# An attention and two-layer FFN kernel on one core: GpSimd's multiplication by 1/sum split by head, and a new table of order offsets

## The chip, the core and the metric

The kernel runs on one core of a Trainium2 chip. The metric is the device time of one execution in microseconds (us). A core has five engines that run side by side: TensorE (PE in the profile; its weight loads are listed as PEld), VectorE (DVE), ScalarE (ACT), GpSimd (POOL) and SyncE (SP), which issues nearly all DMAs here. Each engine takes its instructions strictly in the order of its own queue, so one that waits also holds back everything behind it.

## What is computed

Windowed attention with a few always visible first positions ("sinks"), and behind it two FFN blocks on the 1536 resulting rows. Cut to what matters:

```python
B, H, S, D = 2, 8, 768, 64;  n_sink, window = 4, 128
scores = q @ k.transpose(0, 1, 3, 2) / sqrt(D)
keep = (pos_key < n_sink) | ((0 <= pos_q - pos_key) & (pos_q - pos_key < window))
a = exp(where(keep, scores, -1e9) - max)
a = a / (sum(a) + 1e-9)
x = (a @ v).transpose(0, 2, 1, 3).reshape(1536, 512)
h = x @ w_in1;  g = h if h >= 1, 0 if h <= -1, else (h + 1)**2 / 4;  y = g @ w_out1
h = y @ w_in2;  g = relu(h)**2;  out = g @ w_out2        # d_ff = 2048
```

## The kernel before

**Attention units.** The attention is cut into 24 units (b, j, c): batch b, a block of 256 query rows j = 0..2, a pair of heads c = 0..3. In the names of tiles the numbers are these three, then u (which half of 128 rows) and e (which head of the pair): `p_1_3_0` is the tile p of unit j = 1, c = 3, half u = 0, and holds both heads. A unit goes through these steps:

- SP loads q and k for two units at a time, and v (line 579). PE transposes k and q of a unit into the single PSUM bank `turns` (`turn`, line 660), DVE copies that out as tile k (`turn_copy`, line 674). The next unit can be transposed only when the copy is done. SP moves the last 128 keys of the row block before into place (line 639).
- PE multiplies q by k for each half and head (`scores`, line 690, tiles `s` and `bank`). DVE adds the mask and finds the extreme of each row (`least`, line 699), ACT takes the exponential and the row sum (`powers`, line 707), DVE adds 1e-9 and takes the reciprocal for all four half-and-head sums of the unit (`norm`, lines 713 and 714).
- POOL multiplies the exponentials by 1/sum (`weigh`, line 721), one instruction for a half, over both heads: 2 x 260 columns, or 2 x 128 for the first half of a batch. For j > 0 it then picks the four sink columns out of the product (`sink_cols`, lines 726 and 729).
- PE transposes the product for each head (`turn_p`, line 738, tile `tx`), ACT copies it out (line 745, tile `pt`); the sink columns go the same way (`turn_s`, tile `ts`, lines 751 and 758). PE multiplies by v (line 776, tile `av`), and ACT and DVE write the result into x as a high and a low part (lines 782 and 786).

**FFN.** Every product is done in three matmuls on parts of the operands split into high and low. Weights arrive as 512 KB loads (tile `wraw`, lines 266 and 271). ACT (lines 287, 291, 308), DVE (304, 305, 297, 307) and POOL (309) turn each into its two parts, tile `w`. Hidden products (line 375) go through DVE, ACT and POOL (line 408, tile g) and then into the output products (line 451). While the attention runs, the first FFN steps are mixed in between.

**What sets the order.** `Planner.run` replays the whole program as tasks with costs (`COST`), latencies (`LAG`), waits between kinds of matmuls on PE (`SWITCH`) and buffers (`SLOTS`). At each step it takes the task that can begin first; between tasks that could begin at the same time the smaller key goes first. A key is the unit's number plus an offset for its kind (`KEYS`), plus an entry of `ADJUST` for that one task, by its number. The instructions are then written out in that order, engine by engine. So one changed entry can move many instructions.

Of the kernel before, what the change touches and what calls it, by code (L numbers as in the profile page):

```python
# [17 lines left out]
P = 128  # L18
# [25 lines left out]
    q=2, v=VB, k=KB, p=PB, pt=PTB, sm=4, sp=2, st=2, vs=1, sc=SCB, tp=TPB, tx=TXB, f=PSF,  # L44
# [4 lines left out]
    q=-147.90, v=245.47, kd=-117.22, kp=-240.89, tp=276.69, tpc=83.42, kp0=96.04, s0=-29.55,  # L49
# [12 lines left out]
LEAD = 336.00, 31.97  # L62
LAG = dict(PE=53, ACT=33, DVE=33, POOL=78, SP=40)
COST = dict(
    q=("SP", 2200, 0, 2320), v=("SP", 1100, 0, 1160), kd=("SP", 500, 0, 230), wi=("SP", 500, 0, 1470),
    wo=("SP", 500, 0, 1270), vs=("SP", 900, 0, 200), od=("SP", 500, 0, 800),
    kp=("POOL", 139, 189, 0), kp0=("POOL", 139, 189, 0), vsm=("POOL", 470, 515, 0),
    pm=("POOL", 1006, 1056, 0), pms=("POOL", 562, 615, 0), sp=("POOL", 280, 345, 0),
    cl=("POOL", 1225, 1280, 0), gl=("POOL", 690, 740, 0), gl5=("POOL", 1240, 1290, 0),
    yl=("POOL", 690, 740, 0), yl5=("POOL", 1240, 1290, 0),  # L70
    go=("DVE", 0, 500, 0), gp=("PE", 0, 100, 0),
# [13 lines left out]
)  # L85
FRONT = 137
ADJUST = {
# [4 lines left out]
}  # L92
KIND = dict(s=0, ss=0, tp=1, x=1, xx=6, ts=1, av=2, avv=3, mm=4, mm5=4, vc=5, vl=5)
TAIL = dict(n=92, e=60, es=60, mm5=30)
SWITCH = (
# [3 lines left out]
)  # L99
# [32 lines left out]
class Planner:  # L132
# [5 lines left out]
    def add(self, kind, key, emit, after=(), takes=(), uses=(), count=0, behind=None):  # L138
        n = len(self.tasks)
        t = Task(kind, (key + ADJUST.get(n, 0), n), emit, after, list(takes), list(uses), count)  # L140
        for h in t.uses:
            h.left += 1
        for d in t.after:
            d.next.append((t, False))
        if behind:
            t.after = t.after + [behind]
            behind.next.append((t, True))
        self.tasks.append(t)
        return t
# [439 lines left out]
class Attention:  # L589
# [123 lines left out]
        self.nc.vector.tensor_scalar(sm[:, 1], sm[:, 1], 1.0e-9, None, ALU.add)  # L713
        self.nc.vector.reciprocal(sm[:, 2], sm[:, 1])  # L714

    def weigh(self, b, j, c, u):
        st = self.st[b, j, c]
        wid = P if j + u == 0 else WIN
        s = st["p", u][:, :, :wid]
        r = st["sm"][:, 2, u].unsqueeze(2).broadcast_to([P, 2, wid])  # L720
        self.nc.gpsimd.tensor_tensor(s, s, r, ALU.mult)  # L721

    def sink_cols(self, b, j, c, u):
# [69 lines left out]
    def plan(self, line):  # L793
        add, hold = line.add, Hold
        raw, val, keyh, sinks, self.mask_tasks = {}, {}, {}, {}, {}
        u = {}
        for n, unit in enumerate(UNITS):
# [66 lines left out]
            sp, stt, av = hold("sp"), hold("st"), hold("tx")  # L864
            for i in range(2):
                small = "s" if j + i == 0 else ""
                pm.append(add("pm" + small, key(f"pm{i}"), at(self.weigh, i), [norm], [], [sm]))
                if j > 0:
                    cols.append(
                        add("sp", key(f"sp{i}"), at(self.sink_cols, i), [pm[-1]], [sp][i:], [ph[i]])  # L870
                    )
            turned, ptu = [], []
            few = "x" if j == 0 else ""
            for e in range(2):
                h, pt = hold("tx"), hold("pt")
                t = add(few + "x", key(f"x{e}"), at(self.turn_p, e), pm, [h], ph)
                turned.append(add(few + "xc", key(f"xc{e}"), at(self.turn_p_copy, e), [t], [pt], [h]))
                ptu.append(pt)
            if j > 0:
# [75 lines left out]
def plan_ffn(line, ffn, weights, stage, wtmp, units):  # L955
# [5 lines left out]
    for n, key in enumerate([key for chunks in PASSES for key in chunks]):  # L961
        ps = [key in chunks for chunks in PASSES].index(True)
        raw, ring = [Hold("wr"), Hold("wr")], Hold("w")
        rings[key] = ring
        load = LOADS[n] if n < EARLY else first[ps] - LEAD[0] + 0.1 * PASSES[ps].index(key)
        part = PARTS[n] if n < EARLY else first[ps] - LEAD[1] + 0.1 * PASSES[ps].index(key)
        step = 0.3 if n < EARLY else 0.05
        loads = []
        for h in range(2):
            f = lambda k=key, h=h: weights.load(k, h, stage)  # L970
            before = add("wo" if h else "wi", load + 0.01 * h, f, [before], [raw[h]])
            loads.append(before)
        for h in range(2):
            tmp, last = Hold("wt"), loads[h]
            for i, (kind, f) in enumerate(weights.parts(key, h, wtmp, ring)):
                takes = ([tmp] + [ring] * (h == 0)) if i == 0 else []
                uses = [tmp] * (kind == "cl") + [raw[h]] * (kind in ("ca", "c3"))
                after = [last, begin] if i == 0 else [last]
                after = [last, low] if kind == "c4" else [high] if kind == "c1" else after
                last = add(kind, part + step * h + 0.001 * i, f, after, takes, uses)  # L980
                high, low = last if i == 0 else high, last if i == 1 else low
                begin = last if i == 0 else begin
            parts[key, h] = last
# [358 lines left out]
```

## Time and profile before

| | |
|---|---|
| three runs | 638.45, 639.63, 639.88 us; median 639.63 |
| the profiled execution | 639.68 us, of which the profile's span is 637.6 us |
| TensorE's granted clock | 0.998 of full speed, mean over the span |
| busy share of the span | PE 98%, PEld 80%, DVE 64%, ACT 51%, POOL 48% |
| the chain that ended last | PE 92%, ACT 2%, DVE 2%, POOL 1%, DMA 1% |

How it is read: a share is a mean over stages that differ. The attention of batch 0 lies between about 10 and 65 us, that of batch 1 is mixed with FFN work up to about 173 us, and the rest is FFN alone. A PE that counts as busy may still have waited inside the pipeline, so the times from one start to the next are compared as well.

### The profile page before, as it was taken

The page shows a single profiled execution, that of the slowest core. Times are in us where ns is not written, and L with a number is a line of the kernel's source. Part 1 is how long each engine was busy: PE and PEld are TensorE (multiplying, and loading weights), DVE is VectorE, ACT ScalarE, POOL GpSimd, SP SyncE. Part 2 cuts the span into 40 slices and gives each one's busy share as a digit, 9 for nine tenths or more (in the row PEclk, how much of TensorE's full clock was granted, in tenths as well). Part 3 has the DMA queues.
Part 4 walks back from the last instruction along what each step waited for, and adds up shares of the span by engine and source line. Part 5 has one row for each costly group of instructions (what it writes and reads, how often), then busy time and mean ns, then how long its engine had stood idle before and what let it go on. Part 6 is the DMA issues. An engine that isn't in the chain of part 4 may idle for free.

```text
span 637.6 us, 9207 instructions
## 1 busy us (share of the span) xinstructions
PE 627.8 (98%) x3254; PEld 512.4 (80%) x3254; DVE 410.3 (64%) x855; ACT 324.8 (51%) x695; POOL 305.1 (48%) x334
## 2 busy tenths in 40 slices
PE   8989999999999999999999999999999999999996
PEld 7667788887888887888888888888888888888885
DVE  6888997744478776685498886565664555222222
ACT  4899877654455553554355654555454244211320
POOL 5599487363343543542448873544354144212311
PEclk9999999999999999999999999999999999999999
DMA  6876712300022323223122222223222120001012
GB/s 148 202 202 156 198 50 93 84 1 2 10 89 67 99 67 95 70 67 99 34 67 68 66 67 72 94 67 99 79 87 67 36 96 1 2 1 49 17 66 72
DMA packets 63901, 47.89 MB, mean 75 GB/s; under 512 B 39653, under 2 KB 58341, under 8 KB 63845
## 3 DMA queue, kind: packets, MB, share of 16 engines
q1 hardware_dynamic: 62466, 46.56, 25.5%
q10 hardware_dynamic: 1378, 0.66, 0.4%
q8 instruction: 27, 0.44, 0.3%
q14 instruction: 30, 0.24, 0.1%
HBM read 43.01 MB, written 3.15 MB: 72 GB/s over the span
## 4 chain that ended last, share of the span: by engine, by line
PE 92%; ACT 2%; DVE 2%; POOL 1%; DMA 1%; issue 0%; SPq 0%; DVEq 0%; POOLq 0%; ACTq 0%
PE h L375 25%; PE o L451 20%; PE bank L451 15%; PE bank L375 12%; PE turns L451 7%; PE av L776 3%; PE s L690 3%; PE tx L738 3%; PE turns L375 3%; PE turns L660 1%; ACT p L707 1%; DMA wraw<-in_moe_w_in_dram 1%; PE ts L751 1%; PE bank L899 1%; POOL g L408 0%; DVE p L699 0%
## 5 line engine op out<-in xcount | busy, mean ns | idle before, releaser
L408 POOL TENSOR_TENSOR g<-u,g 128x512 fp32r<-128x512 f32 (+1 forms) x102 | 133.2, 1310 | 168.1 <-ACT g L404 125.5
L375 PE MATMUL h<-x,w 128*128 128x512 f32 x732 | 170.8, 389 | 0.0
L375 PEld LDWEIGHTS h<-x,w 128*128 128x128 f32 x732 | 137.4, 188 | 28.6
L309 POOL TENSOR_TENSOR w<-wx,w 128x512 fp32r<-128x512 f32 x64 | 82.6, 1291 | 123.5 <-ACT w L308 114.6
L404 ACT CAST g<-u 128x512 fp32r<-128x512 f32 (+1 forms) x102 | 60.4, 594 | 58.4 <-DVE u L390 32.3
L375 PE MATMUL bank<-x,w 128*128 128x512 f32 (+1 forms) x420 | 86.9, 356 | 0.0
L308 ACT CAST w<-wx 128x512 fp32r<-128x512 f32 x64 | 39.7, 620 | 81.0 <-DVE wx L307 81.0
L375 PEld LDWEIGHTS bank<-x,w 128*128 128x128 f32 x420 | 69.4, 189 | 11.6 <-DVE u L382 0.3
L304 DVE TENSOR_SCALAR wx<-wx 128x512 f32<-128x512 f32 x64 | 39.6, 619 | 49.7 <-ACT wx L287 49.2
L451 PE MATMUL o<-w,g 128*128 128x512 f32 (+1 forms) x288 | 70.5, 385 | 0.0
L451 PE MATMUL o<-g,w 128*128 128x512 f32 x273 | 67.6, 390 | 0.2 <-POOL g L408 0.2
L451 PE MATMUL bank<-g,w 128*128 128x512 f32 (+1 forms) x324 | 66.2, 345 | 0.0
L451 PEld LDWEIGHTS o<-w,g 128*128 128x128 f32 x288 | 53.4, 188 | 11.3 <-POOL g L408 0.5
L287 ACT ACTIVATE wx<-wraw 128x512 f32<-128x512 f32 x64 | 42.7, 667 | 37.7 <-POOL w L309 36.1
L451 PEld LDWEIGHTS o<-g,w 128*128 128x128 f32 x273 | 51.1, 188 | 11.3 <-POOL g L408 0.6
L451 PEld LDWEIGHTS bank<-g,w 128*128 128x128 f32 x324 | 51.8, 189 | 8.4 <-issue 0.5
L307 DVE CUSTOM_DVE_ANT_0 wx<-wx,wy 128x1024 uint16<-128x1024 uint16 x64 | 56.0, 875 | 2.6
L721 POOL TENSOR_TENSOR p<-p,sm 128x520 f32<-128x520 f32 (+1 forms) x48 | 48.5, 1027 | 18.2 <-DVE sm L714 9.8
L388 ACT ACTIVATE u<-u,half 128x512 f32<-128x512 f32 (+1 forms) x54 | 36.2, 674 | 37.1 <-DVE u L382 37.0
L297 DVE SCALAR_TENSOR_TENSOR wx<-wraw,wx 128x512 int32<-128x512 int32 x64 | 54.2, 847 | 1.1
L490 DVE TENSOR_TENSOR acc<-o,acc 128x512 f32<-128x512 f32 (+1 forms) x50 | 30.0, 605 | 34.7 <-PE o L451 34.6
L390 DVE SCALAR_TENSOR_TENSOR u<-h,u 128x512 f32<-128x512 f32 x37 | 25.4, 687 | 37.5 <-ACT u L384 37.5
(105 smaller groups left out, 853.2 us busy)
## 6 DMA issues: line engine op xcount, KB each, us to landing
wraw<-in_moe_w_in_dram SPq DMA_DIRECT2D x32, 512.0 KB, 3.7
wraw<-in_moe_w_out_dram SPq DMA_DIRECT2D x32, 512.0 KB, 3.5
vr<-in_v_dram SPq DMA_DIRECT2D x24, 128.0 KB, 3.6
qr<-in_q_dram SPq DMA_DIRECT2D x22, 128.0 KB, 3.0
kr<-in_k_dram SPq DMA_DIRECT2D x22, 128.0 KB, 2.8
out_dram<-acc SPq DMA_DIRECT2D x10, 256.0 KB, 2.0
k<-k SPq DMA_DIRECT2D x16, 64.0 KB, 2.1
qr<-in_q_dram SPq DMA_DIRECT2D x4, 64.0 KB, 2.7
```

The costliest lines, as they stand in the source:

```text
L287: nc.scalar.activation(s["x"], f32(s["r"][:, :, 1]), AF.Abs, scale=65536.0)
L297: nc.vector.scalar_tensor_tensor(s["xi"], s["r"][:, :, 1], -(1 << 31), s["xi"], ALU.bitwise_and, ALU.bitwise_or)
L304: ("c1", lambda: nc.vector.tensor_scalar(s["x"], s["x"], 2.0, None, ALU.max)),
L307: ("c4", lambda: nc.vector.tensor_tensor(s["xi"], s["xi"], s["yi"], ALU.add)),
L308: ("cc", lambda: nc.scalar.copy(s["w"][:, 0], s["x"])),
L309: ("cl", lambda: nc.gpsimd.tensor_tensor(s["w"][:, 1], s["x"], f32(s["w"][:, 0]), ALU.subtract)),
L375: nc.tensor.matmul(s["h"], w[:, a, c * P : (c + 1) * P], x[:, b, c, sl], start=n == 0, stop=n == 11)
L388: nc.scalar.activation(s["u"], s["u"], AF.Square, bias=self.half, scale=0.5)
L404: nc.scalar.copy(halves()[0], s["u"])
L408: nc.gpsimd.tensor_tensor(g[1], s["u"], f32(g[0]), ALU.subtract)
L451: nc.tensor.matmul(s["o"], lhs, rhs, start=n + i + j == 0, stop=n == len(chunks) - 1 and i == 1)
L721: self.nc.gpsimd.tensor_tensor(s, s, r, ALU.mult)
```

## The change

Two things are done. `weigh` becomes one POOL instruction for each half and each head (128 x 260 or 128 x 128), with costs to match (569 and 347 ns for the planner where it had 1006 and 562 for two heads). The transposition of head e now waits for the products of head e in both halves, no longer for those of both heads; `sink_cols` waits for both heads of its half. And the planner's numbers change: the first weight load is a kind of its own, `wi0`, whose landing is set 1000 ns later than before; one entry of `SWITCH` goes from 0 to -98; and `ADJUST` has 79 entries where it had 28, all but five of them for tasks of the attention.

```diff
-    pm=("POOL", 1006, 1056, 0), pms=("POOL", 562, 615, 0), sp=("POOL", 280, 345, 0),
+    pm=("POOL", 569, 620, 0), pms=("POOL", 347, 400, 0), sp=("POOL", 280, 345, 0),
...
+    wi0=("SP", 500, 0, 2470),
...
 ADJUST = {
-    209: 325.8, 243: -535.7, 259: -670.5, 348: -90, 353: -1079.1, 387: -240.3, 401: 34.6,
...
+    48: 394.2, 59: 830.871, 74: 1068.43, 96: -879.888, 97: -1091.35, 99: 257.872, 117: 334.328,
...
 SWITCH = (
-    (0, 0, 0, 10, 102, 0, 0, 0), (96, 28, 0, 115, 28, 0, 25, 0), (90, 100, 0, 0, 185, 0, 90, 0),
+    (-98, 0, 0, 10, 102, 0, 0, 0), (96, 28, 0, 115, 28, 0, 25, 0), (90, 100, 0, 0, 185, 0, 90, 0),
...
-    def weigh(self, b, j, c, u):
+    def weigh(self, b, j, c, u, e):
         st = self.st[b, j, c]
         wid = P if j + u == 0 else WIN
-        s = st["p", u][:, :, :wid]
-        r = st["sm"][:, 2, u].unsqueeze(2).broadcast_to([P, 2, wid])
+        s = st["p", u][:, e, :wid]
+        r = st["sm"][:, 2, u, e : e + 1].broadcast_to([P, wid])
         self.nc.gpsimd.tensor_tensor(s, s, r, ALU.mult)
...
             for i in range(2):
                 small = "s" if j + i == 0 else ""
-                pm.append(add("pm" + small, key(f"pm{i}"), at(self.weigh, i), [norm], [], [sm]))
+                for e in range(2):
+                    own = key(f"pm{i}") + 0.001 * e
+                    pm.append(add("pm" + small, own, at(self.weigh, i, e), [norm], [], [sm]))
                 if j > 0:
                     cols.append(
-                        add("sp", key(f"sp{i}"), at(self.sink_cols, i), [pm[-1]], [sp][i:], [ph[i]])
+                        add("sp", key(f"sp{i}"), at(self.sink_cols, i), pm[-2:], [sp][i:], [ph[i]])
                     )
...
-                t = add(few + "x", key(f"x{e}"), at(self.turn_p, e), pm, [h], ph)
+                t = add(few + "x", key(f"x{e}"), at(self.turn_p, e), pm[e::2], [h], ph)
...
-            before = add("wo" if h else "wi", load + 0.01 * h, f, [before], [raw[h]])
+            before = add("wo" if h else "wi" if before else "wi0", load + 0.01 * h, f, [before], [raw[h]])
```

PE, DVE, ACT and SP issue the same instructions as before in another order; POOL issues 48 more. On PE the first 24 rows and the last 1024 (of some 2000) stand as before. The lines of the changed kernel are 9 to 11 higher.

Place 1, POOL, around the products of unit j = 2, c = 0 of batch 0 (line 721, then 730). Before:

```order
L309 TENSOR_TENSOR w_0_580<-wx_0_1_712,w_0_580 128x512
L721 TENSOR_TENSOR p_2_0_1_777<-p_2_0_1_777,sm_2_0_722 128x520
L721 TENSOR_TENSOR p_2_0_0_723<-p_2_0_0_723,sm_2_0_722 128x520
L726 CAST sink_p_252<-p_2_0_1_777 128x2x8
L729 TENSOR_TENSOR sink_p_252<-p_2_0_1_777,sink_p_252 128x8
```

And in the change:

```order
L318 TENSOR_TENSOR w_0_551<-wx_0_1_710,w_0_551 128x512
L730 TENSOR_TENSOR p_1_3_0_604<-p_1_3_0_604,sm_1_3_603 128x260
L658 COPY k_0_1_829<-k_0_1_829 128x4
L735 CAST sink_p_255<-p_1_3_1_750 128x2x8
L738 TENSOR_TENSOR sink_p_255<-p_1_3_1_750,sink_p_255 128x8
L730 TENSOR_TENSOR p_2_0_0_766<-p_2_0_0_766,sm_2_0_765 128x260
L730 TENSOR_TENSOR p_1_3_0_604<-p_1_3_0_604,sm_1_3_603 128x260
L730 TENSOR_TENSOR p_2_0_1_809<-p_2_0_1_809,sm_2_0_765 128x260
L735 CAST sink_p_255<-p_1_3_0_604 128x2x8
```

The two products of two heads are now four of one, and those of the units c = 3 of block 1 and c = 0 of block 2 are mixed.

Place 2, PE, from the scores of unit c = 2 to those of unit c = 3 (block 0, batch 0). Before:

```order
L690 MATMUL s_0_2_0_1_343<-k_0_2_329 128x128
L660 MATMUL turns<-ident,kr_0_2_263 128x128 x2
L660 MATMUL turns<-ident,qr_0_2_260 128x128 x2
L738 MATMUL tx_0_0_0_357<-ident,p_0_0_0_280 128x128
L738 MATMUL tx_0_0_0_357<-ident,p_0_0_1_296 128x128 x2
L738 MATMUL tx_0_0_1_366<-ident,p_0_0_0_280 128x128
L738 MATMUL tx_0_0_1_366<-ident,p_0_0_1_296 128x128 x2
L690 MATMUL bank_64<-k_0_2_329 128x260
L690 MATMUL bank_65<-k_0_2_329 128x260
L690 MATMUL s_0_3_0_0_388<-k_0_3_364 128x128
```

And in the change:

```order
L699 MATMUL s_0_2_0_1_344<-k_0_2_329 128x128
L747 MATMUL tx_0_0_0_349<-ident,p_0_0_0_280 128x128
L747 MATMUL tx_0_0_0_349<-ident,p_0_0_1_296 128x128 x2
L669 MATMUL turns<-ident,kr_0_2_263 128x128 x2
L669 MATMUL turns<-ident,qr_0_2_260 128x128 x2
L747 MATMUL tx_0_0_1_367<-ident,p_0_0_0_280 128x128
L747 MATMUL tx_0_0_1_367<-ident,p_0_0_1_296 128x128 x2
L699 MATMUL s_0_3_0_0_389<-k_0_3_382 128x128
L699 MATMUL s_0_3_0_1_391<-k_0_3_382 128x128
L669 MATMUL turns<-ident,kr_1_0_271 128x128 x2
```

Between the four transpositions of unit c = 3 into `turns` and its first scores there were six transpositions and two scores; now there are three transpositions.

Place 3, SP and ACT, at the first weight load. SP before, and then in the change:

```order
L639 DMA k_2_0_440<-k_1_0_309 128x128
L579 DMA qr_2_0_448<-in_q_dram 128x4x64 x2
L579 DMA kr_2_0_451<-in_k_dram 128x4x64 x2
L266 DMA wraw_0_0_481<-in_moe_w_in_dram 128x4x256
L579 DMA vr_1_2_492<-in_v_dram 128x4x64 x2
```

```order
L648 DMA k_2_0_432<-k_1_0_309 128x128
L275 DMA wraw_0_0_443<-in_moe_w_in_dram 128x4x256
L588 DMA qr_2_0_449<-in_q_dram 128x4x64 x2
L588 DMA kr_2_0_452<-in_k_dram 128x4x64 x2
L588 DMA vr_1_2_482<-in_v_dram 128x4x64 x2
```

ACT before, up to the instruction that reads this load, and then in the change:

```order
L707 ACTIVATE p_1_1_1_526,sm_1_1_510<-p_1_1_1_526,sm_1_1_510 128x260
L782 CAST x<-av_0_2_528 128x256
L707 ACTIVATE p_1_1_1_526,sm_1_1_510<-p_1_1_1_526,sm_1_1_510 128x260
L745 COPY pt_0_3_0_557<-tx_0_3_0_537 128x384
L745 COPY pt_0_3_1_570<-tx_0_3_1_542 128x384
L707 ACTIVATE p_1_1_0_511,sm_1_1_510<-p_1_1_0_511,sm_1_1_510 128x260
L287 ACTIVATE wx_0_0_581<-wraw_0_0_481 128x512
```

```order
L754 COPY pt_0_2_0_519<-tx_0_2_0_504 128x384
L716 ACTIVATE p_1_1_0_540,sm_1_1_539<-p_1_1_0_540,sm_1_1_539 128x260
L296 ACTIVATE wx_0_0_552<-wraw_0_0_443 128x512
L791 CAST x<-av_0_1_527 128x256
L300 ACTIVATE wy_0_0_564<-wraw_0_0_443 128x512
L754 COPY pt_1_0_0_572<-tx_1_0_0_556 128x512
L754 COPY pt_0_2_1_580<-tx_0_2_1_521 128x384
```

On SP the load goes ahead of the q and k loads of block 2. On ACT the instruction that reads it goes ahead of eight: three exponentials, three copies to `pt` and two casts to x.

## Rows read from the trace of the kernel before

**Rows 1.** The page's first part: busy time and share of the engines.

```profile
PE 627.8 (98%) x3254; PEld 512.4 (80%) x3254; DVE 410.3 (64%) x855; ACT 324.8 (51%) x695; POOL 305.1 (48%) x334
```

**Rows 2.** Busy time by stretch: from:to, length, PE, PEld, DVE, ACT, POOL, clock, DMA share, GB/s.

```profile
10.00:26.00 16.00, 15.71 (x126) 11.42 (x125) 14.43 (x65) 14.09 (x55) 9.73 (x17) 1.00 0.73 169
26.00:39.00 13.00, 11.75 (x96) 8.25 (x96) 10.39 (x40) 11.51 (x36) 9.82 (x22) 1.00 0.88 226
39.00:58.00 19.00, 17.45 (x140) 12.93 (x138) 16.62 (x55) 17.30 (x51) 17.36 (x31) 1.00 0.61 150
58.00:100.00 42.00, 42.00 (x338) 34.21 (x337) 38.64 (x121) 35.21 (x104) 28.77 (x42) 1.00 0.52 134
```

**Rows 3.** Timeline of PE at its waits: start, length, instruction, idle before, released by.

```profile
26.41 0.72 PE L690 MATMUL s<-k 64*128 64x260 f32 x4
27.06 0.66 PE L738 MATMUL tx<-ident,p 128*128 128x128 f32 x4
27.55 0.41 PE L751 MATMUL ts<-ident,sink_p 128*96 128x128 f32 x2
27.80 0.60 PE L738 MATMUL tx<-ident,p 128*128 128x128 f32 x4
29.10 0.44 PE L660 MATMUL turns<-ident,kr 128*128 128x128 f32 x2 [0.70 <-DVE k L674]
...
31.13 0.71 PE L690 MATMUL s<-k 64*128 64x260 f32 x4
32.23 0.66 PE L738 MATMUL tx<-ident,p 128*128 128x128 f32 x4 [0.39 <-POOL p L721]
...
40.48 0.71 PE L690 MATMUL s<-k 64*128 64x260 f32 x4
41.72 0.44 PE L660 MATMUL turns<-ident,kr 128*128 128x128 f32 x2 [0.53 <-DVE k L674]
...
45.77 0.71 PE L690 MATMUL s<-k 64*128 64x260 f32 x4
47.13 0.66 PE L738 MATMUL tx<-ident,p 128*128 128x128 f32 x4 [0.65 <-POOL p L721]
...
239.88 0.50 PE L451 MATMUL o<-g,w 128*128 128x512 f32 x1 [0.21 <-POOL g L408]
```

**Rows 4.** Timeline of POOL, the two products of unit j = 2, c = 0.

```profile
45.01 2.07 POOL L721 TENSOR_TENSOR p<-p,sm 128x520 f32<-128x520 f32 x2
```

**Rows 5.** Groups by form, POOL line 721: busy us, mean ns, idle before, releasers.

```profile
L721 POOL TENSOR_TENSOR p<-p,sm 128x520 f32<-128x520 f32 x40 | 43.6, 1105 | 16.5 <-DVE sm L714 8.1 <-ACT p L707 3.5 <-ACT pt L745 2.9
L721 POOL TENSOR_TENSOR p<-p,sm 128x256 f32<-128x256 f32 x8 | 5.1, 636 | 1.7 <-DVE sm L714 1.7
```

**Rows 6.** Line 721 alone by stretch: POOL's busy time, count, clock, DMA.

```profile
26.00:39.00 13.00, 5.44 (x6) 1.00 0.88 226
39.00:58.00 19.00, 8.57 (x8) 1.00 0.61 150
```

**Rows 7.** Groups by form, DVE's copy out of the bank `turns`.

```profile
L674 DVE COPY k<-turns 128x512 f32<-128x512 f32 x23 | 15.7, 685 | 0.8 <-PE turns L660 0.7
```

**Rows 8.** Timeline of ACT ahead of the first weight.

```profile
24.17 0.52 ACT L707 ACTIVATE p<-p,sm 128x260 f32<-128x260 f32 x1
...
24.68 0.84 ACT L745 COPY pt<-tx 128x384 f32<-128x384 f32 x2
...
27.30 0.68 ACT L287 ACTIVATE wx<-wraw 128x512 f32<-128x512 f32 x1 [1.28 <-DMA wraw<-in_moe_w_in_dram]
```

**Rows 9.** SP's issues (timeline), the load's time in the chain, and its size (DMA issues).

```profile
20.03 1.10 SPq L579 DMA_DIRECT2D qr<-in_q_dram  x2
...
22.52 4.76 DMA wraw<-in_moe_w_in_dram
...
wraw<-in_moe_w_in_dram SPq DMA_DIRECT2D x32, 512.0 KB, 3.7
```

More of the change, by code (lines that the diff above doesn't have):

```diff
@@ L64 @@
 COST = dict(
-    q=("SP", 2200, 0, 2320), v=("SP", 1100, 0, 1160), kd=("SP", 500, 0, 230), wi=("SP", 500, 0, 1470),
+    q=("SP", 2200, 0, 2320), v=("SP", 1100, 0, 1160), kd=("SP", 500, 0, 230), wi=("SP", 500, 0, 1470), wi0=("SP", 500, 0, 2470),
     wo=("SP", 500, 0, 1270), vs=("SP", 900, 0, 200), od=("SP", 500, 0, 800),
     kp=("POOL", 139, 189, 0), kp0=("POOL", 139, 189, 0), vsm=("POOL", 470, 515, 0),
-    pm=("POOL", 1006, 1056, 0), pms=("POOL", 562, 615, 0), sp=("POOL", 280, 345, 0),
+    pm=("POOL", 569, 620, 0), pms=("POOL", 347, 400, 0), sp=("POOL", 280, 345, 0),
     cl=("POOL", 1225, 1280, 0), gl=("POOL", 690, 740, 0), gl5=("POOL", 1240, 1290, 0),
```

15 rows, old and new, of the table ADJUST are left out of this document.

## The prediction

> **What bounds the kernel now.** I read the busy shares first: PE is busy for 627.8 us, 98% of the span, and DVE, the next after PE's own weight loads, for 64% [rows 1]. So PE sets the end, and as PE issues the same instructions before and after, only PE's waits can change. The busy time by stretch then says where these lie: PE idles 0.29 us in 10 to 26, 1.25 us in 26 to 39 and 1.55 us in 39 to 58, 3.09 us in all, and nothing from 58 to 100 [rows 2]. In the same stretches ACT is busy 89% and 91%, and POOL 91% in the last: the attention of batch 0 is a pipeline whose stages are nearly all full, so a late step has little room to be made up. The timeline of PE shows each wait and what ended it [rows 3]. Idle time alone tells too little, since the matmul before a wait is still ending; so I take start to start. Two scores that wait for nothing take 0.65 us to the next start (26.41 to 27.06), four transpositions 0.49 us (27.06 to 27.55). The four long waits are then:
>
> - 27.80 to 29.10: 1.30 - 0.49 = 0.81 us, for DVE's copy out of `turns`
> - 31.13 to 32.23: 1.10 - 0.65 = 0.45 us, for POOL's products
> - 40.48 to 41.72: 1.24 - 0.65 = 0.59 us, for DVE's copy
> - 45.77 to 47.13: 1.36 - 0.65 = 0.71 us, for POOL's products
>
> These are 2.56 us. Their idle parts (0.70, 0.39, 0.53, 0.65) are 2.27 of the 3.09 us, so small waits hold another 0.82 us. One more stands in the FFN, 0.21 us of idle time at 239.88. **The ceiling of the gain is 2.56 + 0.82 + 0.21 = 3.59 us**, 0.6% of the time.
>
> **The change, part by part.**
>
> *Products by head, seen by PE.* At 45.01 POOL runs two products of two heads in 2.07 us, and PE begins the transposition of head 0 only when both are done, at 47.13 [rows 3, 4]. Of four products by head, the first two are enough. A product of 520 columns takes 1105 ns and one of 256 takes 636 [rows 5]: a line through both gives 1.78 ns a column and 0.18 us fixed, so 0.64 us for 260. Head 0 is then ready about 2 x 0.64 = 1.29 us after the start, 0.78 us earlier. That covers both POOL waits: **-1.16 us** (0.45 + 0.71), between 0 (if the products themselves begin later) and -1.16.
>
> *Products by head, paid on POOL.* 48 more starts of 0.18 us are 8.7 us of POOL time over the first 173 us. From 58 us on POOL is busy 28.8 of 42 us and PE never idles, which hides them. Between 39 and 58 us eight products are split, 8 x 0.18 = 1.44 us, and POOL's idle time there is 19.00 - 17.36 = 1.64 us: it just fits, and nothing else is left to cover it [rows 2, 6]. The same in 26 to 39: 6 x 0.18 = 1.1 us into 3.2 us. I take **+0.4 us**; bounds 0 and 2.5 (both in full on the path).
> The Trainium skill's GPSIMD Engine Reference, section 3.1 (elementwise cycle accounting), prices a two-operand product at some 2.6 cycles an element, 4497 ns for 2048 elements, and names a software dispatch for each instruction without a figure. By elements alone a split costs nothing, and this term would be zero. The two rows of different width contradict a price by elements alone, and I go by them.
>
> *The order of `turns`.* Both DVE waits come from transposing the next unit into the one bank before the last was copied out; in the new order those two places are other pairs, so 0.81 + 0.59 = 1.40 us go. New ones come: in place 2 the first scores of unit c = 3 stand three transpositions behind the four that fill `turns`. PE needs about 7 x 0.12 = 0.86 us for these seven (0.49 for four), while the scores need the four and then DVE's copy, 0.49 + 0.685 = 1.18 us [rows 7], and DVE is seldom free at once: a new wait of 0.3 us or more, I take 0.5. Further on the new order has two pairs of refills that are closer together than most; I allow 0.4 us. Net **-0.5 us**, bounds -1.4 and +0.3.
>
> *The first weight.* ACT waits 1.28 us for it at 27.30 [rows 8]. It was issued at 22.52 and took 4.76 us; in the new order it is issued where the q load stood, at 20.03, so it lands at 24.8 at the latest, or 23.7 with the median of 3.7 us [rows 9]. But ACT also gets there earlier: three exponentials at 0.51 and three copies at 0.42 no longer stand ahead, 2.8 us less than 26.02, so 23.2 or earlier [rows 8]. ACT then still waits 0.5 to 1.6 us, with other exponentials queued behind it. So I take **0**, bounds -0.8 and +0.3: the wait is moved, not removed.
>
> *What the load passes on SP.* The q and k loads of block 2 are issued 0.55 us later and behind 512 KB, which at 226 GB/s are 2.3 us of the DMA engines' time [rows 2, 9]. PE transposes them at about 26 us. I take **+0.4 us**, bounds 0 and 2.3.
>
> *All other waits* (0.82 + 0.21 us) end in ACT copies, POOL's sink columns and a g of the FFN. All get new neighbours; I take half: **-0.5 us**, bounds -1.0 and +0.5.
>
> Sum: -1.16 + 0.4 - 0.5 + 0 + 0.4 - 0.5 = -1.36 us. Against the profiled execution's 639.68 us that gives **638.3 us**. The median of the runs shown, 639.63, is the same within 0.05.
>
> **The rivals.**
>
> *Nearly all waits go.* The load's passing costs nothing, POOL's extra starts fit, and the new neighbours are better ones. For it: the waits are few and each has a single cause. Against it: ACT and DVE stay as full as they were. The ceiling leaves 639.7 - 3.6 = 636.1; I put this case at 636.4.
>
> *The waits only move.* ACT is 91% busy in 39 to 58 [rows 2], none of its work is removed, and its wait for the weight stays. What PE no longer waits for from POOL it then waits for from ACT a few steps later. The offsets change the order and not the time: 639.6.
>
> *POOL becomes the bound (slower).* Place: 26 to 58 us. 14 products are split there, 14 x 0.18 = 2.5 us [rows 6]. It decides as soon as POOL's idle time between 39 and 58 us, 1.64 us, is used up, for instance because products begin later than before. Then the gain of 1.16 us doesn't come, the starts are on the path and each delays the sinks behind it: +2.5 - 0.5 + 0.4 = +2.4, so 642.1. Against it: 0.2 us are still free, and PE no longer needs the second pair at once.
> The Trainium skill's Perfetto Trace Analysis, "Optimizing Scalar/DVE Operations", speaks of other engines but has both sides of this: group work into larger operations on a saturated engine, and break instructions up where an unsaturated one causes bubbles elsewhere. Taken over to a POOL that is 91% busy, the first half would speak for this rival; the two POOL waits of PE speak for the second half. No row of the kernel before decides it.
>
> **How the numbers follow.** A measurement of this kernel tells changes from about 0.2%, 1.28 us, so faster means below 638.35. The forecast has a chance of 0.55, with its own range 637.0 to 639.3, a good half of it (0.31) below 638.35. Nearly all waits gone 0.15, waits only moved 0.15, POOL the bound 0.15. Faster: 0.31 + 0.15 = 0.46; within 0.2%: 0.24 + 0.15 = 0.39; slower: 0.15. The range of 8 in 10 takes in the forecast, the moved waits and parts of the outer cases: 636.2 to 641.0.
>
> **What would show it.** In the profile after, PE should idle less than 3.09 us between 10 and 58 us, with no wait of `tx` for POOL over 0.3 us; a wait of `s` for DVE's copy near 14 us would confirm place 2; ACT should still wait for the first weight, by 0.5 to 1.6 us near 24; POOL should be busy about 8 us more in all, and over 95% between 39 and 58 us. I am wrong if PE's transpositions of block 2 wait for their loads by more than 1 us, if POOL waits for nothing there and PE for POOL, or if new waits stand in the FFN behind 173 us, where the order moved too.

## The result, and the profile after

| | before | after |
|---|---|---|
| runs | 638.45 to 639.88 us (4) | 642.89 to 643.09 us (4) |
| median | 639.68 us | 643.00 us |
| the profiled execution | 639.68 us | 643.09 us |
| its span, mean granted clock | 637.6 us, 0.998 | 641.0 us, 0.998 |

The change makes the kernel **slower by 3.3 us**: the ratio is 1.0058, with a 95% interval from 1.0046 to 1.0070. The prediction was 638.3 us with a range of 636.2 to 641.0. Sign and range were both wrong; the rival "POOL becomes the bound" (642.1) came nearest.

The first part of the page after, to be held against [rows 1]:

```profile
PE 630.3 (98%) x3254; PEld 512.2 (80%) x3254; DVE 415.7 (65%) x855; ACT 327.1 (51%) x695; POOL 312.4 (49%) x382
```

POOL has its 48 more instructions and 7.3 us more work (312.4 - 305.1). PE has 2.5 us more (630.3 - 627.8) **for the same 3254 instructions**: three quarters of the loss stands in the profile as busy time, not as idle time. (A second profile of the kernel before has 627.0, so 0.8 us of such a difference can be chance.) The busy time by stretch (columns as in [rows 2], and 100 to 173 besides) shows the same from the other side:

```profile
10.00:26.00 16.00, 15.14 (x113) 10.62 (x111) 14.52 (x60) 12.55 (x46) 10.75 (x26) 1.00 0.78 186
26.00:39.00 13.00, 12.11 (x96) 8.10 (x93) 11.88 (x39) 11.93 (x38) 10.74 (x25) 1.00 0.93 231
39.00:58.00 19.00, 18.50 (x151) 13.70 (x152) 16.52 (x55) 17.83 (x54) 17.00 (x35) 1.00 0.56 147
58.00:100.00 42.00, 41.80 (x338) 34.17 (x335) 36.89 (x115) 35.69 (x105) 32.08 (x56) 1.00 0.48 124
100.00:173.00 73.00, 72.42 (x483) 57.31 (x482) 44.98 (x128) 43.00 (x111) 40.05 (x73) 1.00 0.15 43
```

PE idles 0.86 + 0.89 + 0.50 = 2.25 us from 10 to 58 us, less than the 3.09 before, as forecast. The 0.20 and 0.58 us behind that make the sum 3.03: as much as before. Idle time alone would call this kernel equal.

The waits of PE, by what ended them (engine, tile and line; total us, times, longest). The first line is the start of the program and is in every profile here:

```profile
PE bank L910 <- POOL ident masks.py:199: 1.7, 1, 1.7
PE s L699 <- DVE k L683: 0.9, 2, 0.6
PE tx L747 <- POOL p L730: 0.5, 2, 0.3
PE tx L747 <- ACT pt L754: 0.4, 1, 0.4
PE ts L760 <- POOL sink_p L738: 0.4, 1, 0.4
PE o L460 <- POOL g L417: 0.3, 1, 0.3
PE av L785 <- ACT sink_t L767: 0.3, 1, 0.3
PE bank L699 <- DVE sm L708: 0.2, 1, 0.2
```

The two long waits for products [rows 3] are gone; no `tx` waits over 0.3 us for POOL. In their place stand waits for DVE, ACT and the sink columns.

From 170.45 us on before, and from 172.59 in the changed kernel, PE has the same number of matmuls left, 2046, all of the FFN. Up to some 356 us they stand in another order, from there in the same. Counted from the end, the changed kernel is 2.14 us late at the first of them, 1.9 us at 356 us, 2.80 us at PE's last matmul (635.60 against 632.80), and 3.4 us at the end of the span. So **about 2.1 us are lost in the attention**, 0.7 in the FFN, and 0.6 behind PE's last matmul. A loss in the FFN needs no new order: all nine other kernels below that keep PE's order of before lose 0.36 or 0.37 us at one and the same output product (337.26 us in the kernel before), those too that are ahead of it there.

To see the waits that a pipelined PE hides I took, in 10 to 173 us, the time from start to start of each pair of successive matmuls, less the time of the fastest fifth of pairs of the same two kinds in all profiles of this study. Steps more than 0.1 us over that, whose releaser the trace names, add up to (sums of the unrounded figures):

| us, ended by | DVE | ACT | POOL | sum | median time |
|---|---|---|---|---|---|
| before | 3.3 | 1.0 | 1.6 | 5.9 | 639.7 |
| after | 4.4 | 1.4 | 2.0 | 7.8 | 643.0 |
| split in the old order | 2.1 | 0.8 | 4.4 | 7.3 | 642.2 |
| small POOL instructions added | 3.5 | 0.7 | 3.7 | 7.9 | 642.8 |
| split, low sink part left out | 3.6 | 1.2 | 1.2 | 5.9 | 639.5 |
| after, addition left out | 2.9 | 2.4 | 0.7 | 5.9 | 641.3 |
| fitted order, two heads, 2nd | 3.8 | 0.0 | 0.2 | 4.0 | 634.8 |

The 1.9 us between the first two rows are nearly all of the 2.14. But how a step is put down to an engine matters: if only the waits of the matmul itself count, and not those of the weight load ahead of it, the POOL column stays the same within 0.1 us, while DVE has 2.3 before and 2.3 after, ACT 0.4 and 1.3, and the sum rises by 1.3 us. So POOL's column can be leaned on, DVE's rise of 1.1 us cannot.

The other rows are the experiments that follow. Ratios there are to the kernel before on the same chip, and each has its own runs of it (medians 638.96 to 639.38).

### The profile page after: what moved, and what is told of

It is laid out like the page before. It is cut to its first block, busy times and chain, and to the rows that moved or that the text cites. A ratio compares the mean times of both kernels' runs of the same rounds, so it can differ in the third digit from the quotient of the medians.

```text
span 641.0 us, 9251 instructions
## 1 busy us (share of the span) xinstructions
PE 630.3 (98%) x3254; PEld 512.2 (80%) x3254; DVE 415.7 (65%) x855; ACT 327.1 (51%) x695; POOL 312.4 (49%) x382
## 5 line engine op out<-in xcount | busy, mean ns | idle before, releaser
L384 PE MATMUL h<-x,w 128*128 128x512 f32 x696 | 162.1, 389 | 0.0
L384 PEld LDWEIGHTS h<-x,w 128*128 128x128 f32 x696 | 130.7, 188 | 27.1
L384 PE MATMUL bank<-x,w 128*128 128x512 f32 (+1 forms) x492 | 104.1, 361 | 0.1
L384 PEld LDWEIGHTS bank<-x,w 128*128 128x128 f32 x492 | 82.9, 189 | 15.6 <-issue 0.8
L460 PE MATMUL o<-w,g 128*128 128x512 f32 (+1 forms) x300 | 73.6, 386 | 0.3 <-POOL g L417 0.3
L460 PE MATMUL o<-g,w 128*128 128x512 f32 x279 | 70.5, 389 | 0.0
L730 POOL TENSOR_TENSOR p<-p,sm 128x260 f32<-128x260 f32 (+1 forms) x96 | 59.8, 647 | 18.3 <-DVE sm L723 16.0
L460 PE MATMUL bank<-g,w 128*128 128x512 f32 (+1 forms) x300 | 60.0, 341 | 0.0
L460 PEld LDWEIGHTS bank<-g,w 128*128 128x128 f32 x300 | 47.2, 189 | 7.6 <-DVE acc L497 0.7
L716 ACT ACTIVATE p<-p,sm 128x260 f32<-128x260 f32 (+1 forms) x96 | 47.0, 493 | 8.0 <-DVE sm L708 7.5
```

What stands on the lines that cost most here:

```text
L384: nc.tensor.matmul(s["h"], w[:, a, c * P : (c + 1) * P], x[:, b, c, sl], start=n == 0, stop=n == 11)
L460: nc.tensor.matmul(s["o"], lhs, rhs, start=n + i + j == 0, stop=n == len(chunks) - 1 and i == 1)
L716: self.nc.scalar.activation(s, s, AF.Exp, bias=sm[:, 0, u, e : e + 1], scale=-1.0, accum_out=sm[:, 1, u, e : e + 1])
```

## The experiments

**1. The split alone, in the old order.** In `weigh` of the kernel before:

```diff
-        s = st["p", u][:, :, :wid]
-        r = st["sm"][:, 2, u].unsqueeze(2).broadcast_to([P, 2, wid])
-        self.nc.gpsimd.tensor_tensor(s, s, r, ALU.mult)
+        for e in range(2):
+            s = st["p", u][:, e, :wid]
+            r = st["sm"][:, 2, u, e : e + 1].broadcast_to([P, wid])
+            self.nc.gpsimd.tensor_tensor(s, s, r, ALU.mult)
```

> The kernel before with one edit: each product of two heads is written as two products of one head at the same place; no order, offset or cost is changed. Theory P (POOL is the bound in the attention: each extra start of 0.18 us makes POOL's products and sink columns later, and that is the whole loss): slower than before by 2 to 3.5 us, 641.7 to 643.2 us. Theory O (the split is about neutral and the new offsets are a worse order): within 1 us of before, 638.7 to 640.7, and the prediction's own terms for the split alone (-1.16 + 0.4) would give 638.9.

Measured: 642.23 us, ratio 1.0051 (1.0031 to 1.0072). **The split alone costs 3.3 us**, as theory P said. The order of every engine is that of before, so each matmul can be compared with itself. PE's timeline:

```profile
46.21 0.66 PE L739 MATMUL tx<-ident,p 128*128 128x128 f32 x4 [1.09 <-POOL p L722]
46.70 0.38 PE L660 MATMUL turns<-ident,kr 128*128 128x128 f32 x2
46.92 0.38 PE L660 MATMUL turns<-ident,qr 128*128 128x128 f32 x2
48.74 0.42 PE L752 MATMUL ts<-ident,sink_p 128*96 128x128 f32 x2 [1.44 <-POOL sink_p L730]
```

and POOL's:

```profile
44.19 2.72 POOL L722 TENSOR_TENSOR p<-p,sm 128x260 f32<-128x260 f32 x4
46.86 0.66 POOL L727 CAST sink_p<-p 128x16 fp32r<-128x16 f32 x1
47.59 0.20 POOL L730 TENSOR_TENSOR sink_p<-p,sink_p 128x8 f32<-128x8 f32 x1
47.74 0.66 POOL L727 CAST sink_p<-p 128x16 fp32r<-128x16 f32 x1
48.48 0.20 POOL L730 TENSOR_TENSOR sink_p<-p,sink_p 128x8 f32<-128x8 f32 x1
```

The same `ts` before, and the sink columns ahead of it on POOL:

```profile
48.43 0.42 PE L751 MATMUL ts<-ident,sink_p 128*96 128x128 f32 x2 [0.21 <-POOL sink_p L729]
...
47.02 0.40 POOL L726 CAST sink_p<-p 128x16 fp32r<-128x16 f32 x1
47.49 0.20 POOL L729 TENSOR_TENSOR sink_p<-p,sink_p 128x8 f32<-128x8 f32 x1
47.64 0.46 POOL L726 CAST sink_p<-p 128x16 fp32r<-128x16 f32 x1
48.17 0.20 POOL L729 TENSOR_TENSOR sink_p<-p,sink_p 128x8 f32<-128x8 f32 x1
```

At the first `tx` of the split PE is 0.92 us ahead of [rows 3] (47.13), and POOL begins its four products 0.82 us ahead of [rows 4] (45.01). They take 2.72 us where the pair took 2.07, and the sink columns end at 48.68, where they ended at 48.37. PE needs them for `ts`, which before began at 48.43 and now at 48.74. The lead is gone at one step: **the wait for the products has become a wait for the sink columns behind them.** Of the 1.13 us by which POOL's chain is longer there, 0.65 are the products; the rest is in the two casts, 0.66 us each where they took 0.40 and 0.46, for a reason that no run here shows. Further losses of 0.59 us (a `tx` at 58.32, for products) and 0.32 us (a `ts` at 113.56) end in POOL too. In this profile PE's last matmul is 1.6 us late, and 1.1 us more lie behind it; those are not waits for POOL (last section).

**2. Head 0 first.** The changed kernel's tasks with the orders of before, written out as a list that the planner must follow, and in 15 units the products in the order head 0, head 0, head 1, head 1:

```diff
                 for t in tasks:
+                    if t.key[1] != given[e][0]:
+                        continue
                     at = self.starts(t, free)
```

> The changed kernel's tasks (products by head, head e transposed after its own two products) in the order of the kernel before on every engine; where the two halves' products stand next to each other on POOL (15 of 24 units) they go head 0, head 0, head 1, head 1. Theory P: POOL has the same 48 starts, so it is as slow as the split in the old order, within 0.5 us (641.7 to 643.2). The prediction's mechanism (head 0 ready 0.78 us earlier ends PE's two waits for POOL): at least 0.8 us faster than the split in the old order.

Measured: 642.20 us, ratio 1.0044 (1.0031 to 1.0057): no faster than the first, so the prediction's mechanism doesn't pay even where head 0 goes ahead in both halves. The waits of PE say why:

```profile
PE ts L898 <- POOL sink_p L876: 2.4, 2, 2.2
...
PE tx L885 <- POOL p L868: 0.3, 1, 0.3
```

The waits for products are 0.3 us (1.0 before) and those for sink columns 2.4 (0.2 before). The `ts` that began at 48.43 before, and at 48.74 in experiment 1, begins at 49.26 here. What follows on it differs from experiment 1, since in this profile the clock falls behind that wait (last section).

**3. Head 0 first where PE waited, and nowhere else.** In `weigh` of the kernel before:

```diff
+        parts = [(u, slice(0, 2))]
+        if (b, j, c) in ((0, 1, 1), (0, 2, 0)):
+            parts = [(1, slice(0, 1))] if u else [(0, slice(0, 1)), (1, slice(1, 2)), (0, slice(1, 2))]
+        for u, e in parts:
```

> The kernel before with products by head in two units alone, those for which PE waited for POOL before (j = 1, c = 1 and j = 2, c = 0 of batch 0), in the order head 0, head 0, head 1, head 1; 4 extra starts, 0.7 us of POOL. The prediction's mechanism alone (both waits of PE for products vanish): 1.16 us faster, 637.8 to 638.5. If PE then waits for the sink columns of the same unit instead: within 0.5 us of before.

Measured: 639.83 us, ratio 1.0007 (0.9996 to 1.0017): no gain. This run shows the term of the prediction and its undoing side by side, in PE's timeline:

```profile
31.71 0.66 PE L742 MATMUL tx<-ident,p 128*128 128x128 f32 x4
32.97 0.39 PE L780 MATMUL av<-sink_t,vs 96*128 96x256 f32 x1 [0.61 <-ACT pt L749]
...
46.33 0.66 PE L742 MATMUL tx<-ident,p 128*128 128x128 f32 x4
...
49.09 0.42 PE L755 MATMUL ts<-ident,sink_p 128*96 128x128 f32 x2 [1.67 <-POOL sink_p L733]
```

Both `tx` start without a wait. Against the same matmuls before, PE gains 0.46 us at the first and 0.72 us at the second: 1.18 us, where the prediction had 1.16. A step later the first 0.45 us go to a wait for ACT's copy, and 2.8 us later 1.46 us go to the sink columns.

**4. POOL's time without the split.** A copy of 4 columns on a tile of its own behind each of the 48 products of two heads:

```diff
         self.nc.gpsimd.tensor_tensor(s, s, r, ALU.mult)
+        self.nc.gpsimd.tensor_copy(self.pad[:, 4:8], self.pad[:, :4])
```

> The kernel before, products of two heads, with one more small POOL instruction (a copy of 4 columns on a tile of its own, no data of the kernel) behind each of the 48 products: as many extra POOL starts as the split has, about 0.14 to 0.19 us each by the rows of the 4 and 8 column copies, but nothing of the split's earlier head 0. Theory P (the extra POOL time in the attention is the loss): 2 to 4 us slower than before. If something else of the split costs (its waits, its order): within 1 us of before.

Measured: 642.76 us, ratio 1.0048 (1.0031 to 1.0065). POOL's groups by form (busy us, mean ns, idle before) give the copies:

```profile
L724 POOL COPY pad<-pad 128x4 f32<-128x4 f32 x48 | 14.3, 299 | 0.0
```

and the page's first part POOL's sum:

```profile
PE 630.1 (98%) x3254; PEld 513.6 (80%) x3254; DVE 412.0 (64%) x855; ACT 326.0 (51%) x695; POOL 312.3 (49%) x383
```

POOL is busy 312.3 us, as in the changed kernel (312.4), and the time is the same. The copies took 299 ns where 140 to 190 were expected, 14.3 us in all; the sum rose by 7.2 only, because other POOL rows were shorter. So **POOL's time alone, 7 us more of it spread over the attention, is enough for a loss as large as that of the split**; its waits and its order are not needed to explain it. Part of the loss came by way of the clock (last section). The Trainium skill's GPSIMD Engine Reference gives in section 3.1 a price per element and, for the dispatch of an instruction on GpSimd, no figure. The copies of 4 columns take 299 ns here, which a price per element alone would miss.

**5. POOL's time given back.** The second instruction of `sink_cols` is taken out, in three kernels:

```diff
-        self.nc.gpsimd.tensor_tensor(t[:, 1], p, t[:, 0], ALU.subtract)
```

In the split with the old order:

> The split in the old order, without the second instruction of the sink columns (the low part of the sink weights is left out): POOL has the 48 extra starts (8.7 us) and 32 instructions less (6.7 us). Theory P: most of the loss of the split goes, 638.5 to 640. If POOL's time is not the cause: it stays above 641.5.

In the kernel before and in the changed kernel:

> The kernel before without the second instruction of the sink columns (the low part of the sink weights is left out, 32 POOL instructions, 6.7 us of POOL time by the row of 210 ns each); the order of all else is kept. Theory P: POOL is not the bound before, so the gain is small, 0 to 1.2 us (638.5 to 639.7). Theory O: the same gain as in the changed kernel, whatever it is.

> The changed kernel without the second instruction of the sink columns (the same part left out, 32 POOL instructions, 7.8 us of POOL time at 244 ns each), order kept. Theory P: this gives POOL back about what the split took, so most of the loss goes: 2 us or more faster than the changed kernel, 639.8 to 641.0, and the gap to the kernel before without the same instruction closes to under 1.5 us. Theory O: the gap stays near 3.3 us.

Measured: 639.52 us, ratio 1.0000 (0.9990 to 1.0010), for the split: its loss is gone. The kernel before gains little (638.43; 0.9989, 0.9980 to 0.9999). But the **changed kernel gains 0.8 us and no more** (642.24; 1.0046, 1.0029 to 1.0062, which overlaps with the 1.0046 to 1.0070 that it had): theory P, as far as it was to explain the changed kernel, was wrong there. With POOL relieved, the new order is 2.7 us slower than the old one with the same split (642.24 against 639.52). So POOL's time is not what holds most of the loss in the new order. (The instruction taken out stands itself in the chain to the sink columns, as the added starts and copies do; these runs don't tell POOL's total time from the length of that chain.) The table above points to what does: against the split in the old order, the new order has brought POOL's share down from 4.4 to 2.0 us, and DVE's and ACT's up from 2.9 to 5.8 (from 1.4 to 3.6 without the waits of weight loads).

**6. Time off DVE.** That was then tried: the addition of 1e-9 to the row sums is left out.

```diff
-        self.nc.vector.tensor_scalar(sm[:, 1], sm[:, 1], 1.0e-9, None, ALU.add)
```

> The changed kernel without the addition of 1e-9 to the row sums (24 DVE instructions of 128x4, 5.4 us of DVE in the rows; that addition is left out). Theory D (in the new order PE's waits that end in DVE and ACT hold the loss; giving POOL back 7.8 us brought only 0.8): 1 us or more faster than the changed kernel, 640.5 to 642. If the loss there is neither POOL's nor DVE's: within 0.5 us of it.

> The split in the old order, without the same addition. There POOL bounds, and DVE is not what PE waits for (its waits for POOL are twice those for DVE): theory D expects less than in the changed kernel, 0 to 0.8 us, 641.4 to 642.3. A gain as large as in the changed kernel would speak against it: the addition also stands in the chain ahead of POOL's products.

> The kernel before without the same addition, as the base of the two others: 0 to 1 us faster than before, 638.4 to 639.4.

Measured: the changed kernel 641.27 us (1.0030, 1.0018 to 1.0041), 1.7 us less than with it; the split in the old order 642.27 (1.0045, 1.0028 to 1.0061), unchanged; the kernel before 638.86 (0.9997, 0.9988 to 1.0007). So the two slow kernels are not slow for the same reason: **in the old order POOL binds; in the new one the chain through DVE holds more than POOL's own time does.** Whether it is DVE's time stays open: the addition also stands in the chain ahead of POOL's products, and in the table POOL's share falls by 1.3 us along with DVE's 1.5, while ACT's rises by 1.0. The profile of the split without the addition shows the fall of the clock (last section), that of experiment 1 doesn't; this may hide a small gain, but not one of 1.7 us, as the fastest runs, 641.51 and 641.76, lie close too.

**7. The first weight load ahead, alone.** On SP the load goes ahead of the q and k loads of block 2, in the order of before:

```diff
             order = fast_plan(at, ffn, weights, stage, wtmp)
+            w = order.index(next(t for t in order if t.kind == "wi"))
+            q = max(n for n in range(w) if order[n].kind == "q")
+            order.insert(q, order.pop(w))
```

> The kernel before with one move: on SP the first weight load is issued ahead of the q and k loads of block 2, as in the changed kernel; every engine's order is else kept. If ACT's wait of 1.28 us for this load reaches PE, and q and k still land in time: 0.4 to 0.9 us faster than before. By the prediction's own terms (0 for the wait, +0.4 for what the load passes): within 0.5 us of before, on the slow side.

Measured: 638.66 us, ratio 0.9992 (0.9982 to 1.0001): a small gain or none. ACT's timeline, against [rows 8]:

```profile
26.04 0.69 ACT L287 ACTIVATE wx<-wraw 128x512 f32<-128x512 f32 x1
```

The wait of 1.28 us is gone, and PE stands 1.2 us ahead of before at 31.8 us; 0.36 us of that are lost in the FFN, at the output product named above.

**8. Other orders.** Two orders were searched by moving single tasks in the planner's own replay, after its prices had been set to the trace: `sink_cols` is planned with 345 ns from start to end (280 to the next start), and its two instructions take 484 and 482 ns in the median of the two traces. The new prices are 482 ns and 424 to the next start.

```diff
-    sp=("POOL", 280, 345, 0),
+    sp=("POOL", 424, 482, 0),
```

> The kernel before with products of two heads, and another order on all five engines, found by moving single tasks in the planner's replay after its prices were set to the trace: sink columns 424 ns a step and 482 ns in all (the table has 280 and 345; the two instructions take 247 + 244 ns in the rows), the first landing 1000 ns later, -98 between scores. If PE's waits are a matter of order: 3 to 6 us faster than before, 633 to 636. If the replay's other errors eat the gain: 638 to 640.

> The changed kernel's products by head, in an order found in the same way with the same prices. Theory P (the split's 48 starts load POOL, but an order that knows the true price of POOL's work can hide them): within 1 us of the fitted order with two heads. If the split costs in any order: 2 us or more slower than that one. Against the changed kernel: at least 4 us faster if its loss lies in order and prices.

> As the fitted order with two heads, with a longer search in the same replay and the same prices. If the replay still ranks orders rightly: about 1 us faster than that one, 634 to 635.5. If its errors (up to 0.9 us against the chip) decide: the same as that one within 0.5 us.

Measured: products of two heads 635.69 us (0.9949, 0.9932 to 0.9966), by head 637.27 (0.9973, 0.9961 to 0.9984), and two heads with the longer search **634.79 us (0.9927, 0.9911 to 0.9944)**, 4.6 us faster than before and 1.3% faster than the changed kernel. Its waits of PE:

```profile
PE bank L1034 <- POOL ident masks.py:199: 1.7, 1, 1.7
PE turns L795 <- DVE k L809: 1.3, 2, 0.8
PE tx L873 <- DVE x L921: 0.6, 1, 0.6
PE bank L825 <- DVE k L809: 0.2, 1, 0.2
```

Behind the start it lists no wait for POOL. (8 warm-up matmuls of the start are not issued in the fitted orders; PE has 3246 instructions.) By head is 1.6 us slower than the first order with two heads, from a search of the same length, between the two forecasts (under 1, over 2). So also where an order is made for it the split shows no gain; it is one search each, and the 1.6 us are no clean price. How much of the 4.6 us comes from the prices and how much from the search was not separated.

**9. How far one profile can be trusted.** The kernel before, once more:

> The kernel before, unchanged, for a second profile of it: how far two executions of one program lie apart at PE's first scores, at the end of the attention, and from PE's last instruction to the end of the span. Expected: PE within 0.5 us, the end within 0.6 us.

Measured: 639.69 us, span 637.6. PE's last matmul ends within 0.1 us of that in the first profile; in the first 8 us single matmuls start up to 0.6 us apart. Behind the first 8 us, differences of a few tenths at the same matmul are therefore read as differences of the kernels. It is one pair, and a fall of the clock, as in the last section, is no part of it.

## Why the prediction was wrong

*Products by head, seen by PE (-1.16).* The size was right, 1.18 us in experiment 3, and the two waits are gone in the changed kernel. What failed is that I counted a wait removed as time gained, without asking what PE needs next from the same engine: four transpositions into `turns` behind `tx`, PE needs the sink columns, which stand behind all four products on POOL. The prediction's list had this rule only for the rival.

*Products by head, paid on POOL (+0.4; "it just fits, and nothing else is left to cover it").* **This is the step that failed.** That the starts fit into 1.64 us of idle time was the mistake. Idle time of POOL isn't free where it comes from: half of it ahead of the products stood where POOL waited for DVE's 1/sum [rows 5], while the added time stands in the chain from the products to the sink columns. The price measured in the old order is 3.3 us, and 3.4 for 48 small instructions without the split. That is beyond my bound of 2.5, which held only the splits between 26 and 58 us; losses followed at 58 and 114 us. I had taken "PE never idles from 58 to 100" [rows 2] for a cover. The size of a start was low as well. The products after:

```profile
L730 POOL TENSOR_TENSOR p<-p,sm 128x260 f32<-128x260 f32 x80 | 52.4, 677 | 18.2 <-DVE sm L723 15.8 <-PE ts L760 0.9 <-ACT wx L296 0.7
L730 POOL TENSOR_TENSOR p<-p,sm 128x128 f32<-128x128 f32 x16 | 7.8, 500 | 0.2 <-DVE sm L723 0.2
```

They take 60.2 us where they took 48.7 [rows 5], 0.24 us for each added start and not 0.18; POOL's sum rose by 7.3 us only because other rows, the casts of the sink columns above all, got shorter. The rival with the right place and mechanism (each start "delays the sinks behind it") had a chance of 0.15.

*The sign by which I wanted to see it* failed with it: POOL was to be over 95% busy in 39 to 58 us, and is at 17.00 of 19, 89%, in the changed kernel and at 17.07, 90%, in the split in the old order, where it does bind. An engine needs no full stretch to bind; it needs to be last at one step of the chain, again and again.

*The order of `turns` (-0.5).* Place 2 came as forecast, in PE's timeline after:

```profile
14.54 0.49 PE L699 MATMUL s<-k 64*128 64x128 f32 x4 [0.56 <-DVE k L683]
...
36.99 0.63 PE L747 MATMUL tx<-ident,p 128*128 128x128 f32 x4 [0.27 <-POOL p L730]
...
40.36 0.63 PE L747 MATMUL tx<-ident,p 128*128 128x128 f32 x4 [0.44 <-ACT pt L754]
...
162.99 0.38 PE L785 MATMUL av<-sink_t,vs 96*128 96x256 f32 x1 [0.26 <-ACT sink_t L767]
...
495.53 0.50 PE L460 MATMUL o<-w,g 128*128 128x512 f32 x1 [0.26 <-POOL g L417]
```

0.56 us of idle time for the 0.5 I took, and the two old waits for DVE's copy are gone. But the net was wrong: the steps that end in DVE did not shrink by 0.5 us. They grew by 1.1 us in the table, or stayed the same without the waits of weight loads.

*The first weight (0; ACT still waits 0.5 to 1.6 us).* Wrong in the mechanism. ACT's timeline after has no wait there:

```profile
24.00 0.51 ACT L716 ACTIVATE p<-p,sm 128x260 f32<-128x260 f32 x1 [0.66 <-DVE sm L708]
24.41 0.19 ACT L716 ACTIVATION_READ_ACCUMULATOR p<-p,sm 128x1 f32 x1
24.51 0.66 ACT L296 ACTIVATE wx<-wraw 128x512 f32<-128x512 f32 x1
```

ACT comes at 24.51 and finds the load there. I had it at 23.2 or earlier, because I took instructions off its queue and didn't ask what the rest waits for: here, 0.66 us, for DVE. Alone the move is worth 0 to 1 us (experiment 7).

*What the load passes (+0.4).* No wait of PE for a load is listed after; the term is 0.

*All other waits (-0.5).* Wrong in sign. In the attention new neighbours brought waits for ACT (0.44 and 0.26 us in the rows above), and the FFN, which before had 0.21 us [rows 3], lost 0.7 us against before, with the longest wait at 495.53. PE's order is the same in both kernels there. About half of the 0.7 us is no more than what the kernels in the old order lose in the FFN too.

So in the old order the sum should have read about +3.3: nothing gained for the two waits, and the starts at eight times what I took. For the changed kernel the account is not complete. Its time is that of the split in the old order (1.0051 and 1.0058, no difference can be told), but not its mechanism: with POOL relieved its ratio goes no further than from 1.0058 to 1.0046, and the -1.0 us that I took for `turns` and all other waits did not come. The new order with products of two heads was not run, so how much of the 3.3 us the split costs there, and how much the offsets, stays open. That the rival's 642.1 lies near is luck in part: it had POOL's 2.5 us in its sum, where the new order shows 2.0 us of steps that end in POOL against 1.6 before.

## What to carry to other kernels

A wait that ends in a nearly full engine isn't gained by serving its consumer earlier; follow that engine's queue to the next thing the consumer needs from it, and price the added starts there, not against the engine's idle time. Where a replay sets the order, compare its prices with the trace first (one was 28% low here); an order searched after that was 4.6 us faster than before, though prices and search were not told apart. And compare start to start: PE's busy time for the same instructions rose by 2.5 us while its idle time didn't change.

## What was not expected

*The clock after a wait.* In experiment 2 the `ts` at 49.26 ended an idle time of 2.19 us:

```profile
49.26 0.42 PE L898 MATMUL ts<-ident,sink_p 128*96 128x128 f32 x2 [2.19 <-POOL sink_p L876]
```

The windows behind it (columns as in [rows 2]; the clock is the third number from the end):

```profile
48.00:49.00 1.00, 0.00 (x0) 0.00 (x0) 0.83 (x3) 0.00 (x0) 0.84 (x4) 1.00 0.36 94
49.00:50.00 1.00, 0.74 (x5) 0.62 (x7) 0.00 (x0) 0.28 (x2) 1.00 (x5) 0.84 0.55 103
50.00:51.00 1.00, 1.00 (x8) 0.62 (x8) 0.00 (x0) 1.00 (x5) 0.61 (x2) 0.50 1.03 362
51.00:52.00 1.00, 1.00 (x10) 0.67 (x8) 0.00 (x0) 0.31 (x2) 0.00 (x0) 0.50 0.23 75
52.00:53.00 1.00, 1.00 (x5) 0.34 (x4) 0.52 (x2) 0.67 (x2) 0.26 (x1) 0.50 0.10 24
53.00:54.00 1.00, 1.00 (x7) 0.83 (x7) 1.00 (x5) 0.33 (x1) 1.00 (x2) 0.95 0.91 205
```

The clock fell to 0.50, the lower level of 1.2 GHz, after the wait and stayed there for over 3 us; PE's lag against before grew in that time from 0.82 to 2.24 us, and was 2.0 us later on. The kernel with the added copies shows the same behind its two waits there (clock 0.68 over 49 to 54 us), and so does the split without the addition (0.57 over 49 to 53 us). The changed kernel doesn't, nor do the profiles of experiments 1 and 3, though PE waited 1.44 and 1.67 us for the sink columns there. In three profiles, then, a wait for POOL was paid twice; in the others it was not.

*The end of the program.* Behind PE's last matmul the span goes on for 4.8 us before, 5.4 after and 5.9 in the split in the old order, though all engines issue the same instructions there. The row of the last matmuls of the split, whose span is 640.3 us:

```profile
633.25 1.12 PE L451 MATMUL bank<-w,g 128*128 128x256 f32 x8
```

Both profiles of the kernel before have 4.8 to 4.9, the changed kernel and the same without the low sink part 5.4. In the split nearly all of the difference lies between two of POOL's closing instructions, its last drain and the semaphore event behind it: 1.2 us there, under 0.1 us before. The split's starts do not explain it: head 0 first, with as many, has 4.9, and the kernel with the added copies 5.0. Whether it goes with the program or with the single execution is not shown, as only the kernel before was profiled twice; its cause stays open. In the profile of experiment 1 it is 1.1 of the 2.6 us by which the span is longer; with the low sink part left out the split has 6.0 and still reaches the time of before.
